# A decode step bound by its weight stream: new stream order, regrouped first layer of the MLP, smaller weight pieces, zero fill on VectorE, eight K/V buffers

## Chip, cores, metric

The kernel runs on one core of one Trainium2 chip. The metric is the device time of one execution in microseconds (us). Kernels that are compared ran on the same chip in alternating rounds. A ratio is the mean time of one kernel's fast runs over that of the other's of the same rounds, so it is not quite the ratio of the medians quoted beside it. The record calls a run faster or slower only beyond 2 %; a smaller difference is named below when its interval excludes 1.

In the profile lines PE is TensorE (the matmuls), DVE is VectorE, ACT ScalarE, POOL GpSimd, and SPq the queue in which the engine SP issues its loads (DMAs). PSUM is the memory, divided into banks, that matmuls add their results into.

## The reference, cut to what matters

```python
# one token, D = 576; 32 query heads, 16 K/V heads, Dh = 128; the last 4096 of 32768 cached positions
q = x @ wq                                   # 576 x 4096
p = softmax(q . K * Dh**-0.5)                # K: 16 heads x 4096 x 128
a = (p . V) @ wo                             # V the same; wo: 4096 x 576
b = gelu(x @ w1 + b1) @ w2 + b2              # w1: 576 x 4608, w2: 4608 x 576
out = g * a + (1 - g) * b                    # g = sigmoid(sum(x * gate_w))
```

There is one row of activations, so every weight and cache byte is used once: 53.6 MB are read, of which K and V are 33.6 MB and each of the four weight matrices about 5 MB.

## The kernel before

All large loads are issued by one engine (SP) in the order wq, K (16 tiles of 1 MiB), w1, V (16 tiles), wo, w2. K and V tiles share seven buffers. PE consumes wq (q), then each K tile (VectorE transposes it first), then, after the softmax, the MLP's first layer from w1, then V, then wo and w2 row by row.

```python
kv_pool = ctx.enter_context(tc.tile_pool(name="kv_pool", bufs=7, side="right"))
nc.gpsimd.memset(qz_flat, 0.0)                       # 128 x 8320 bf16
# ... q, then scores of 16 K tiles, softmax -> pt ...
first = True                                          # first layer of the MLP
for j in range(NJ):                                   # NJ = 18
    for half in range(2):
        col, f0 = half * NJ + j, half * FH + j
        for k in range(KM):                           # 4 matmuls, 128 rows of weights
            matmul(h_ps[:, col:col+1], lhsT=w1_m[:, k, f0:(half+1)*FH:NJ], rhs=xt[:, k:k+1], ...)
        matmul(h_ps[:, col:col+1], lhsT=b1_row[0:1, f0:(half+1)*FH:NJ], rhs=one_b, ...)   # bias: 1 row
    matmul(h_ps[:, j:NF:NJ], lhsT=w1_l[:, j:FH:NJ], rhs=xl[:, 0:2], ...)                  # last 64 rows of w1
for h in range(Hkv):                                  # V: load a tile, 32 matmuls of 2 columns
    ...
for r in range(0, RO, 16):                            # wo in two pieces
    nc.sync.dma_start(out=wo_t[:, r:r+16, :], in_=wo_src[:, r:r+16, :])
cuts = [(0, 0, 18), (1, 0, 9), (1, 9, 15), (1, 15, 18)]        # w2: rows per piece
# ... then one pair of matmuls (512 and 64 columns) for each of 32 rows of wo and 36 of w2, and
nc.scalar.copy(out=out_row[:, 320:D], in_=y_ps[0:1, 320:D])
nc.vector.tensor_copy(out=out_row[:, 0:320], in_=y_ps[0:1, 0:320])
nc.sync.dma_start(out=out, in_=out_row)
```

## Time and profile before

| | before |
|---|---|
| time, median | 144.57 us (144.55 to 144.71, 3 runs) |
| span of the profiled run | 142.9 us |
| bytes read, mean rate | 53.6 MB, 375 GB/s |
| PE, VectorE busy | 67 %, 39 % |
| last byte of w2 / end of the last matmul | 136.3 us (DMA records of the trace) / 139.4 us |

The page cuts the span into 40 slices, here of 3.57 us. The first line is the clock that TensorE was granted, in tenths; the second is what the DMA engines moved.

```profile
PEclk9999999999999999985555555555555555599998
...
GB/s 161 420 431 420 422 413 424 415 424 417 424 410 426 408 446 428 423 418 415 417 417 420 417 163 73 429 413 433 404 436 399 450 412 454 402 429 411 314 11 3
```

The stream runs at about 420 GB/s from the second slice on. Two things break it: slices 24 and 25 (163 and 73), the *hole*, and the *tail*, the last two slices, in which next to nothing is loaded. The shares of busy time say nothing of this: PE is busy 67 % of the span, but mostly in the shadow of the stream.

One caution about the clock line: the first clock record in the trace stands at 25.9 us, and where there is none the page shows 9. Before it TensorE was in fact at half clock: the 512-column matmuls of the K stage follow each other every 0.43 us up to 25.7 us, and every 0.22 us from 26.0 us on.

The view of what SP's queue waited for has the hole's cause (total us, times, longest):

```profile
SPq L342 <- PE o_ps L347: 22.9, 9, 16.3
```

Loads of V wait for PE to finish with a buffer, once for 16.3 us. What PE does in that time is the first layer. In PE's timeline (start, duration, engine, line, what) one group of columns looks so:

```profile
69.28 0.22 PE L304 MATMUL h_ps<-xl,w_t 128*128 128x2 bf16 x1
69.36 0.39 PE L287 MATMUL h_ps<-xt,w_t 128*128 128x1 bf16 x4
69.69 0.22 PE L296 MATMUL h_ps<-one_b,b_row 1*128 1x1 bf16 x1
69.83 0.41 PE L287 MATMUL h_ps<-xt,w_t 128*128 128x1 bf16 x4
70.17 0.22 PE L296 MATMUL h_ps<-one_b,b_row 1*128 1x1 bf16 x1
70.33 0.22 PE L304 MATMUL h_ps<-xl,w_t 128*128 128x2 bf16 x1
```

L287 is the loop over k, L296 the bias, L304 the last rows. A group of 11 matmuls repeats every 1.05 us (69.28 to 70.33), 18 times. The layer ends, V begins and the loads resume only here:

```profile
85.97 0.22 PE L304 MATMUL h_ps<-xl,w_t 128*128 128x2 bf16 x1
...
86.06 5.10 PE L347 MATMUL o_ps<-pt,kv_t 128*128 128x2 bf16 x186
...
87.08 3.74 SPq L342 DMA_DIRECT2D kv_t<-in_A_v_cache_dram  x5
```

The tail, in the chain that ended last (start, duration, what released what):

```profile
100.79 29.66 DMA w_t<-in_B_w_dram
130.49 0.38 PE y_ps L165
...
139.51 0.37 ACT out_row L390
139.90 0.48 DVE out_row L391
```

The first w2 piece (18 of 36 rows, 2.6 MB) lets PE go at 130.49 us; from there 36 row pairs of 0.245 us follow, then two copies and the store. The view of waits (total us, times, longest):

```profile
PE y_ps L165 <- DMA wo_t<-in_A_wo_dram: 3.4, 1, 3.4
...
PE y_ps L165 <- DMA w_t<-in_B_w_dram: 0.7, 1, 0.7
```

PE lost 3.4 us before its first row of wo, which came only with a piece of 16 rows, and 0.7 us before w2.

Last, two small VectorE copies beside the zero fill on GpSimd (busy us, mean ns | idle before):

```profile
L110 POOL MEMSET early<- 128x8320 bf16 x1 | 7.0, 7035 | 0.0
L120 DVE COPY xd<-x_row 1x64 bf16<-1x64 bf16 x2 | 6.0, 5908 | 1.0 <-DMA x_row<-in_A_x_dram 1.0
```

The Trainium skill, page "SBUF — State Buffer", section "SBUF: two separate sides", says that VectorE and GpSimd share one pair of ports as an exclusive lock: in some modes the later of two instructions waits for the whole of the other. The trace agrees: 64 elements took 5.9 us here, until 8.00 us, just after the fill's end at 7.92. That these copies were in such a mode is not shown by itself.

### The profile page before, as it was taken

What the parts mean: (1) busy time and instruction counts of PE and PEld (TensorE: products, weight loads), DVE (VectorE), ACT (ScalarE), POOL (GpSimd) and SP (SyncE); (2) the same over time, 40 slices, a digit from 0 to 9 for tenths busy, and PEclk for the clock granted to TensorE, in tenths of its full rate; (3) what the DMA queues carried; (4) which work ended last, traced back from release to release, by engine and by line L of the source; (5) the groups of instructions that cost most, each with busy time, mean ns of one, the idle gap of its engine ahead of it and who ended that gap; (6) DMA issues with size and microseconds to landing.
All of it is one profiled execution on the core that took longest, in us unless ns stands there. A gap on an engine that the chain in (4) does not pass through costs nothing.

```text
span 142.9 us, 2520 instructions
## 1 busy us (share of the span) xinstructions
PE 95.9 (67%) x1140; PEld 60.2 (42%) x1140; DVE 55.8 (39%) x82; ACT 3.8 (3%) x8; POOL 7.7 (5%) x7
## 2 busy tenths in 40 slices
PE   0049639988867868624999999933342507998990
PEld 0034513333323323213899999933342502343440
DVE  4968297899998989446000004000000030000001
ACT  3000000000000000020000000000000000000001
POOL 8920000000000000000000000000000000000000
PEclk9999999999999999985555555555555555599998
DMA  4999999999999999999999933999999999999700
GB/s 161 420 431 420 422 413 424 415 424 417 424 410 426 408 446 428 423 418 415 417 417 420 417 163 73 429 413 433 404 436 399 450 412 454 402 429 411 314 11 3
DMA packets 6645, 53.79 MB, mean 376 GB/s; under 512 B 741, under 2 KB 745, under 8 KB 1257
## 3 DMA queue, kind: packets, MB, share of 16 engines
q1 hardware_dynamic: 6626, 53.61, 90.5%
q8 instruction: 9, 0.15, 0.4%
q14 instruction: 2, 0.02, 0.0%
q10 hardware_dynamic: 8, 0.01, 0.0%
HBM read 53.62 MB, written 0.00 MB: 375 GB/s over the span
## 4 chain that ended last, share of the span: by engine, by line
DMA 57%; PE 30%; DVE 10%; issue 1%; ACT 1%; ACTq 0%
DMA w_t<-in_B_w_dram 38%; DMA kv_t<-in_A_k_cache_dram 10%; DMA kv_t<-in_A_v_cache_dram 8%; PE h_ps L287 7%; PE y_ps L165 7%; PE s_ps L228 4%; DVE xd L120 4%; PE h_ps L296 4%; DVE early L224 3%; PE o_ps L347 2%; PE h_ps L304 2%; PE q_ps L178 2%; PE y_ps L168 1%; DMA x_row<-in_A_x_dram 1%; DVE junk_row L135 0%
## 5 line engine op out<-in xcount | busy, mean ns | idle before, releaser
L228 PE MATMUL s_ps<-early 128*128 128x512 bf16 x128 | 32.8, 403 | 10.5 <-DVE early L224 10.5
L224 DVE STREAM_TRANSPOSE early<-kv_t 128x2048 f32<-128x2048 f32 x16 | 36.6, 2304 | 3.7 <-DMA kv_t<-in_A_k_cache_dram 2.1
L228 PEld LDWEIGHTS <-early 128*128 128x128 bf16 x128 | 12.9, 101 | 30.0 <-issue 17.9
L347 PE MATMUL o_ps<-pt,kv_t 128*128 128x2 bf16 x512 | 15.2, 165 | 13.0 <-DMA kv_t<-in_A_v_cache_dram 10.4
L347 PEld LDWEIGHTS <-kv_t 128*128 128x128 bf16 x512 | 14.5, 104 | 13.7 <-DMA kv_t<-in_A_v_cache_dram 10.9
L287 PE MATMUL h_ps<-xt,w_t 128*128 128x1 bf16 x144 | 14.5, 204 | 1.7 <-DMA w_t<-in_B_w_dram 1.7
L165 PE MATMUL y_ps<-wo_t,ov 128*1 128x512 bf16 x32 | 10.9, 470 | 3.4 <-DMA wo_t<-in_A_wo_dram 3.4
L287 PEld LDWEIGHTS <-w_t 128*128 128x128 bf16 x144 | 12.3, 160 | 2.0 <-DMA w_t<-in_B_w_dram 1.8
L371 DVE COPY o_sb<-o_ps 128x32 f32<-128x32 f32 x1 | 0.2, 192 | 25.8 <-PE o_ps L347 25.8
L391 DVE CAST out_row<-y_ps 1x320 bf16<-1x320 f32 x1 | 0.5, 478 | 24.1 <-ACT out_row L390 24.1
L165 PE MATMUL y_ps<-w_t,gt 128*1 128x512 bf16 x36 | 9.0, 380 | 0.7 <-DMA w_t<-in_B_w_dram 0.7
L296 PE MATMUL h_ps<-one_b,b_row 1*128 1x1 bf16 x36 | 7.8, 217 | 0.0
L313 DVE COPY hacc<-h_ps 128x36 f32<-128x36 f32 x1 | 0.2, 195 | 18.5 <-PE h_ps L304 18.5
L110 POOL MEMSET early<- 128x8320 bf16 x1 | 7.0, 7035 | 0.0
L168 PE MATMUL y_ps<-wo_t,ov 128*1 128x64 bf16 x32 | 6.9, 217 | 0.0
L168 PE MATMUL y_ps<-w_t,gt 128*1 128x64 bf16 x36 | 6.9, 193 | 0.0
L120 DVE COPY xd<-x_row 1x64 bf16<-1x64 bf16 x2 | 6.0, 5908 | 1.0 <-DMA x_row<-in_A_x_dram 1.0
L165 PEld LDWEIGHTS <-ov 128*1 128x1 bf16 x32 | 3.2, 100 | 6.6 <-issue 3.8
L296 PEld LDWEIGHTS <-b_row 1*128 1x128 bf16 x36 | 4.9, 135 | 0.5
L165 PEld LDWEIGHTS <-gt 128*1 128x1 bf16 x36 | 3.0, 84 | 4.7
L304 PE MATMUL h_ps<-xl,w_t 128*128 128x2 bf16 x18 | 4.0, 223 | 0.5 <-DMA w_t<-in_B_w_dram 0.5
L168 PEld LDWEIGHTS <-ov 128*1 128x1 bf16 x32 | 3.0, 94 | 3.0 <-issue 3.0
(75 smaller groups left out, 39.4 us busy)
## 6 DMA issues: line engine op xcount, KB each, us to landing
kv_t<-in_A_k_cache_dram SPq DMA_DIRECT2D x16, 1024.0 KB, 15.3
kv_t<-in_A_v_cache_dram SPq DMA_DIRECT2D x16, 1024.0 KB, 18.9
w_t<-in_B_w_dram SPq DMA_DIRECT2D x2, 2304.0 KB, 20.5
wo_t<-in_A_wo_dram SPq DMA_DIRECT2D x2, 2304.0 KB, 25.9
wq_t<-in_A_wq_dram SPq DMA_DIRECT2D x4, 1024.0 KB, 7.9
w_t<-in_B_w_dram SPq DMA_DIRECT2D x1, 2592.0 KB, 29.7
w_t<-in_B_w_dram SPq DMA_DIRECT2D x1, 1296.0 KB, 30.3
w_t<-in_B_w_dram SPq DMA_DIRECT2D x1, 864.0 KB
```

The source lines that it names most:

```text
L110: nc.gpsimd.memset(qz_flat, 0.0)
L120: nc.vector.tensor_copy(out=xd[:, :, t], in_=x_row[0:1, DM:D])
L165: nc.tensor.matmul(y_ps[0:1, 0:N0], lhsT=vec, rhs=row[:, 0:N0], start=start, stop=stop, skip_group_check=True)
L168: nc.tensor.matmul(y_ps[0:1, N0:D], lhsT=vec, rhs=row[:, N0:D], start=start, stop=stop, skip_group_check=True)
L178: nc.tensor.matmul(q_ps[:, j : j + 1], lhsT=wq_m[:, k, j * Dh : (j + 1) * Dh], rhs=xt[:, k : k + 1], start=(k == 0 and j == 0), stop=False ...
L224: nc.vector.transpose(out=kt.bitcast(FP32), in_=k_t[:].bitcast(FP32))
L228: nc.tensor.matmul(s_ps[:, f * 512 : (f + 1) * 512].rearrange("p (c k) -> p c k", k=32), lhsT=qz[:, h, j, :], rhs=kv[:, f * 16 : (f + 1) * ...
L287: nc.tensor.matmul(h_ps[:, col : col + 1], lhsT=w1_m[:, k, f0 : (half + 1) * FH : NJ], rhs=xt[:, k : k + 1], start=first, stop=False, skip ...
L296: nc.tensor.matmul(h_ps[:, col : col + 1], lhsT=b1_row[0:1, f0 : (half + 1) * FH : NJ], rhs=one_b[0:1, 0:1], start=False, stop=False, skip ...
L304: nc.tensor.matmul(h_ps[:, j:NF:NJ], lhsT=w1_l[:, j:FH:NJ], rhs=xl[:, 0:2], start=False, stop=(j == NJ - 1), skip_group_check=True,)
L347: nc.tensor.matmul(o_ps[:, 2 * h : 2 * h + 2], lhsT=v_t[:, c, :], rhs=pt[:, c, 2 * h : 2 * h + 2], start=(c == 0), stop=(c == NCH - 1),)
L391: nc.vector.tensor_copy(out=out_row[:, 0:320], in_=y_ps[0:1, 0:320])
```

## The change

Its intent is to keep the stream full: the first layer moves to where PE has nothing else to do, V follows the softmax at once, and the last pieces are small so that little work is left after the last byte. There are several edits at once.

1. Stream order w1, wq, K, V, wo, w2, and the first layer is computed first.
2. w1 in four pieces and a rest, wo in four pieces in place of two, w2 in six in place of four.
3. The loop nest of the first layer is regrouped: all 36 bias matmuls, then for each k all 36 columns, then the 18 of the last rows.
4. The zero fill goes from GpSimd to VectorE.
5. Eight K/V buffers. wo and w2 take over other tiles (tags A and B in place of C and A), which makes room.

```diff
-    kv_pool = ... bufs=7
+    kv_pool = ... bufs=8
+    for k in range(KM):                                   # before wq now
+        nc.sync.dma_start(out=w1_m[:, k, :], in_=w1_src[:, k, :])
-    nc.gpsimd.memset(qz_flat, 0.0)
+    nc.vector.memset(qz_flat.bitcast(FP32), 0.0)
+    for c in range(NF):                                   # before q now; 36 columns
+        f0 = (c // NJ) * FH + c % NJ
+        matmul(h_ps[:, c:c+1], lhsT=b1_row[0:1, f0:(c//NJ+1)*FH:NJ], rhs=one_b, start=(c == 0), ...)
+    for k in range(KM):
+        for c in range(NF):
+            matmul(h_ps[:, c:c+1], lhsT=w1_m[:, k, f0:(c//NJ+1)*FH:NJ], rhs=xt[:, k:k+1], ...)
+    for j in range(NJ):
+        matmul(h_ps[:, j:NF:NJ], lhsT=w1_l[:, j:FH:NJ], rhs=xl[:, 0:2], ...)
     ... (gelu as before; the old nest and the old loads of w1 go) ...
-    for r in range(0, RO, 16):
+    for r in range(0, RO, 8):
-    cuts = [(0, 0, 18), (1, 0, 9), (1, 9, 15), (1, 15, 18)]
+    cuts = [(0, 0, 9), (0, 9, 18), (1, 0, 8), (1, 8, 13), (1, 13, 16), (1, 16, 18)]
```

More of the change, by code (lines that the diff above doesn't have):

```diff
@@ L52 @@
     big = ctx.enter_context(tc.tile_pool(name="big", bufs=1, side="right"))
-    kv_pool = ctx.enter_context(tc.tile_pool(name="kv_pool", bufs=7, side="right"))
+    kv_pool = ctx.enter_context(tc.tile_pool(name="kv_pool", bufs=8, side="right"))
     ps_s = ctx.enter_context(tc.tile_pool(name="ps_s", bufs=1, space=bass.MemoryType.PSUM))
@@ L68 @@
     nc.scalar.dma_start(out=b1_row[:], in_=B_b1.rearrange("(o n) -> o n", o=1))
+    w1_t = big.tile([P, KM * F + FH], BF16, name="w1_t", tag="B")
+    w1_m = w1_t[:, 0 : KM * F].rearrange("p (k n) -> p k n", k=KM)
+    w1_l = w1_t[:, KM * F :]
+    w1_src = B_w1[0:DM, :].rearrange("(p k) n -> p k n", k=KM)
+    for k in range(KM):
+        nc.sync.dma_start(out=w1_m[:, k, :], in_=w1_src[:, k, :])
+    nc.sync.dma_start(out=w1_l, in_=B_w1[DM:D, :].rearrange("r (two n) -> (r two) n", two=2))
     wq_t = big.tile([P, KM * Hq * Dh + QH], BF16, name="wq_t", tag="A")
@@ L172 @@
     y_add(one_f[0:1, 0:1], b2g[0:1, :], start=True)
+    h_ps = ps_h.tile([P, NF], FP32, name="h_ps")
+    for c in range(NF):
+        f0 = (c // NJ) * FH + c % NJ
+        nc.tensor.matmul(
+            h_ps[:, c : c + 1],
+            lhsT=b1_row[0:1, f0 : (c // NJ + 1) * FH : NJ],
+            rhs=one_b[0:1, 0:1],
+            start=(c == 0),
+            stop=False,
+            skip_group_check=True,
+        )
+    for k in range(KM):
+        for c in range(NF):
+            f0 = (c // NJ) * FH + c % NJ
+            nc.tensor.matmul(
+                h_ps[:, c : c + 1],
+                lhsT=w1_m[:, k, f0 : (c // NJ + 1) * FH : NJ],
+                rhs=xt[:, k : k + 1],
+                start=False,
+                stop=False,
+                skip_group_check=True,
+            )
+    for j in range(NJ):
+        nc.tensor.matmul(
+            h_ps[:, j:NF:NJ],
+            lhsT=w1_l[:, j:FH:NJ],
+            rhs=xl[:, 0:2],
+            start=False,
+            stop=(j == NJ - 1),
+            skip_group_check=True,
+        )
+    hacc = const.tile([P, NF], FP32, name="hacc")
+    nc.vector.tensor_copy(out=hacc[:], in_=h_ps[:])
+    z2 = const.tile([P, NF], FP32, name="z2")
+    nc.vector.tensor_tensor(out=z2[:], in0=hacc[:], in1=hacc[:], op=ALU.mult)
+    C0 = 0.7978845608028654
+    poly = const.tile([P, NF], FP32, name="poly")
+    nc.vector.tensor_scalar(
+        out=poly[:],
+        in0=z2[:],
+        scalar1=2.0 * C0 * 0.044715,
+        scalar2=2.0 * C0,
+        op0=ALU.mult,
+        op1=ALU.add,
+    )
+    u_t = const.tile([P, NF], FP32, name="u_t")
+    nc.vector.tensor_tensor(out=u_t[:], in0=poly[:], in1=hacc[:], op=ALU.mult)
+    e_h = const.tile([P, NF], FP32, name="e_h")
+    nc.scalar.activation(out=e_h[:], in_=u_t[:], func=ACT.Exp, scale=-1.0)
+    nc.vector.tensor_scalar(out=e_h[:], in0=e_h[:], scalar1=1.0, scalar2=None, op0=ALU.add)
+    r_t = const.tile([P, NF], FP32, name="r_t")
+    nc.vector.reciprocal(out=r_t[:], in_=e_h[:])
+    p1 = const.tile([P, NF], FP32, name="p1")
+    nc.vector.tensor_tensor(out=p1[:], in0=hacc[:], in1=r_t[:], op=ALU.mult)
+    gt = const.tile([P, NF], BF16, name="gt")
+    nc.vector.tensor_scalar(out=gt[:], in0=p1[:], scalar1=omg[:, 0:1], scalar2=None, op0=ALU.mult)
     q_ps = ps_m.tile([P, Hq], FP32, name="q_ps", tag="m")
@@ L235 @@
                 )
-    w1_t = big.tile([P, KM * F + FH], BF16, name="w1_t", tag="B")
-    w1_m = w1_t[:, 0 : KM * F].rearrange("p (k n) -> p k n", k=KM)
-    w1_l = w1_t[:, KM * F :]
-    w1_src = B_w1[0:DM, :].rearrange("(p k) n -> p k n", k=KM)
-    for k in range(0, KM, 2):
-        nc.sync.dma_start(out=w1_m[:, k : k + 2, :], in_=w1_src[:, k : k + 2, :])
-    nc.sync.dma_start(out=w1_l, in_=B_w1[DM:D, :].rearrange("r (two n) -> (r two) n", two=2))
     m1 = const.tile([P, 1], FP32, name="m1")
@@ L277 @@
     nc.vector.transpose(out=pt[:].rearrange("p c h -> p (c h)"), in_=p_t[:])
-    h_ps = ps_h.tile([P, NF], FP32, name="h_ps")
-    first = True
-    for j in range(NJ):
-        for half in range(2):
-            col = half * NJ + j
-            f0 = half * FH + j
-            for k in range(KM):
-                nc.tensor.matmul(
-                    h_ps[:, col : col + 1],
-                    lhsT=w1_m[:, k, f0 : (half + 1) * FH : NJ],
-                    rhs=xt[:, k : k + 1],
-                    start=first,
-                    stop=False,
-                    skip_group_check=True,
-                )
-                first = False
-            nc.tensor.matmul(
-                h_ps[:, col : col + 1],
-                lhsT=b1_row[0:1, f0 : (half + 1) * FH : NJ],
-                rhs=one_b[0:1, 0:1],
-                start=False,
-                stop=False,
-                skip_group_check=True,
-            )
-        nc.tensor.matmul(
-            h_ps[:, j:NF:NJ],
-            lhsT=w1_l[:, j:FH:NJ],
-            rhs=xl[:, 0:2],
-            start=False,
-            stop=(j == NJ - 1),
-            skip_group_check=True,
-        )
@@ L312 @@
-    hacc = const.tile([P, NF], FP32, name="hacc")
-    nc.vector.tensor_copy(out=hacc[:], in_=h_ps[:])
-    z2 = const.tile([P, NF], FP32, name="z2")
-    nc.vector.tensor_tensor(out=z2[:], in0=hacc[:], in1=hacc[:], op=ALU.mult)
-    C0 = 0.7978845608028654
-    poly = const.tile([P, NF], FP32, name="poly")
-    nc.vector.tensor_scalar(
-        out=poly[:],
-        in0=z2[:],
-        scalar1=2.0 * C0 * 0.044715,
-        scalar2=2.0 * C0,
-        op0=ALU.mult,
-        op1=ALU.add,
-    )
-    u_t = const.tile([P, NF], FP32, name="u_t")
@@ L327 @@
-    nc.vector.tensor_tensor(out=u_t[:], in0=poly[:], in1=hacc[:], op=ALU.mult)
-    e_h = const.tile([P, NF], FP32, name="e_h")
-    nc.scalar.activation(out=e_h[:], in_=u_t[:], func=ACT.Exp, scale=-1.0)
-    nc.vector.tensor_scalar(out=e_h[:], in0=e_h[:], scalar1=1.0, scalar2=None, op0=ALU.add)
-    r_t = const.tile([P, NF], FP32, name="r_t")
-    nc.vector.reciprocal(out=r_t[:], in_=e_h[:])
-    p1 = const.tile([P, NF], FP32, name="p1")
-    nc.vector.tensor_tensor(out=p1[:], in0=hacc[:], in1=r_t[:], op=ALU.mult)
@@ L335 @@
-    gt = const.tile([P, NF], BF16, name="gt")
-    nc.vector.tensor_scalar(out=gt[:], in0=p1[:], scalar1=omg[:, 0:1], scalar2=None, op0=ALU.mult)
     o_ps = ps_o.tile([P, Hq], FP32, name="o_ps")
@@ L356 @@
     RO = Hq * Dh // P
-    wo_t = big.tile([P, RO, D], BF16, name="wo_t", tag="C")
+    wo_t = big.tile([P, RO, D], BF16, name="wo_t", tag="A")
     wo_src = A_wo.rearrange("(p r) n -> p r n", r=RO)
-    for r in range(0, RO, 16):
-        nc.sync.dma_start(out=wo_t[:, r : r + 16, :], in_=wo_src[:, r : r + 16, :])
-    w2_t = big.tile([P, NF, D], BF16, name="w2_t", tag="A")
+    for r in range(0, RO, 8):
+        nc.sync.dma_start(out=wo_t[:, r : r + 8, :], in_=wo_src[:, r : r + 8, :])
+    w2_t = big.tile([P, NF, D], BF16, name="w2_t", tag="B")
     w2_src = B_w2.rearrange("(b p j) n -> p b j n", b=2, j=NJ)
-    cuts = [(0, 0, 18), (1, 0, 9), (1, 9, 15), (1, 15, 18)]
+    cuts = [(0, 0, 9), (0, 9, 18), (1, 0, 8), (1, 8, 13), (1, 13, 16), (1, 16, 18)]
     for b, j0, j1 in cuts:
```

## The prediction

> **What bounds it now.** The weight and cache stream. The page's slices show about 420 GB/s from 4 to 132 us (53.6 MB, the 16 DMA engines full). The rest of the 142.9 us span is a start of 2 us, one hole, and a tail.
> - Hole: slices 24 and 25 (82 to 89 us) show 163 and 73 GB/s; (677 / 420) x 3.57 = 5.1 us of stream lost (estimate). In the SP waits V loads wait for PE on o_ps (22.9 us, longest 16.3). PE is in the MLP's first layer from 66.8 to 86.0 us (timeline: 11 matmuls per 1.04 us), consumes no V tile, all 7 buffers fill, loads stop.
> - Tail: the DMA records end at 136.3 us, but the first 2.6 MB piece of w2 releases PE only at 130.49 (chain of waits). 36 row pairs at 0.245 us then run PE-bound to 139.4; copies and store take 3.45 us more.
>
> **What the change does.**
> 1. The first layer moves to the front, in the stream's shadow. PE passes straight from softmax to V. With V0 finished near 81 us and V7 landing near 86, V8 is issued in time: the hole closes, -5.1 us.
> 2. w2 lands in six pieces, the last of 3 and 2 rows. PE's 0.245 us a row beats the stream's (147 KB / 420 GB/s = 0.35 us), so only the last rows remain after the last byte: 0.5 us to the first matmul (first w2 piece: bytes end 129.98, matmul 130.49), then about 0.6. This tail shrinks from 3.1 us to 1.1: -2.0 us.
> 3. VectorE's zero fill replaces GpSimd's 7.04 us memset, beside which two VectorE copies of 64 elements took 5.98 us (line groups). x is ready 3 to 5 us sooner; not critical.
> 4. Added delay: q comes after w1. PE first does 36 bias matmuls (0.14 us each), 144 strided ones (0.083) and the fp32 bias row (2.1): q is ready at 32 to 34 us, though wq lands at 26. K starts 4 us behind, but a backlogged K tile needs 2.19 us, the stream 2.5, and eight buffers hold 20 us. It is absorbed; K ends at 71 to 73 us.
> 5. Bytes and matmuls are the same.
>
> The Trainium skill, "TensorE: Matmul & The Clock Gate", Part 1, says that an idle PE falls to half clock and takes a busy window to return. The trace agrees: granted clock 0.5 from 63.4 to 124.8 us; one- and two-column matmuls did not lift it, it rose 5.9 us after the 512-column wo matmuls began (0.48 us a row before, 0.245 after). This stays: wo starts near 109 us, falls 12 rows behind, and catches up by 125, before the bytes end.
>
> **Sum.** Stream end 136.3 - 5.1 = 131.2 us; +0.5 landing, +0.6 matmuls, +3.45 end = 135.8 us span. Times are 1.7 us above the span: 137.5 us, 0.951 of before. Range 136.0 to 139.6. Chances: faster by over 2% 0.94, within 2% 0.05, slower 0.01.
>
> **Right if:** slices from 4 to 129 us are all near 420 GB/s; V loads wait little on PE; the chain ends in w2's DMA, two to five rows, copies; K transposes start at 32 to 36 us.
>
> **Wrong if:** V0 ends after 86 us (a smaller hole returns); PE stays at half clock into w2 (up to 5 us more); small last pieces slow the stream or land unevenly over the 16 engines.

## The result and the profile after

| | before | after |
|---|---|---|
| time, median | 144.64 us (144.55 to 144.91, 4 runs) | 137.97 us (137.96 to 138.04, 4 runs) |
| ratio | | 0.9537 (95 % interval 0.9521 to 0.9554) |
| span | 142.9 us | 136.1 us |
| mean rate | 375 GB/s | 394 GB/s |
| last byte of w2 / end of the last matmul | 136.3 / 139.4 us | 131.7 / 133.2 us |

The span is 6.8 us shorter. The last byte comes 4.6 us earlier (the hole), and from the last byte to the end of the last matmul it is 1.5 us in place of 3.1 (the tail). The same two lines of slices, now of 3.40 us:

```profile
PEclk9999999999999999999999655555555555799999
...
GB/s 122 423 425 421 420 419 419 408 420 412 421 421 424 419 417 421 419 417 424 419 421 414 419 421 424 412 421 412 417 421 414 427 427 406 433 417 426 403 182 0
```

No slice between the second and the 38th is under 403 GB/s. SP's longest wait for PE on V is now 10.2 us, in a time in which enough loads are queued already:

```profile
SPq L341 <- PE o_ps L346: 14.3, 8, 10.2
```

The start of the program, all engines:

```profile
7.71 2.39 PE L187 MATMUL h_ps<-one_b,b_row 1*128 1x1 bf16 x36 [0.25 <-DMA b_row<-in_B_b_dram]
...
10.03 4.64 PE L198 MATMUL h_ps<-xt,w_t 128*128 128x1 bf16 x72
...
16.61 4.64 PE L198 MATMUL h_ps<-xt,w_t 128*128 128x1 bf16 x72
...
21.11 1.26 PE L207 MATMUL h_ps<-xl,w_t 128*128 128x2 bf16 x18
...
22.23 1.84 PE L245 MATMUL q_ps<-xt,wq_t 128*128 128x1 bf16 x64
...
27.35 1.01 PE L245 MATMUL q_ps<-xt,wq_t 128*128 128x1 bf16 x32 [1.69 <-DMA wq_t<-in_A_wq_dram]
...
30.95 2.31 DVE L291 STREAM_TRANSPOSE early<-kv_t 128x2048 f32<-128x2048 f32 x1 [0.41 <-DMA kv_t<-in_A_k_cache_dram]
```

The layer's matmuls are the same 198, but 36, 72, 72 and 18 of them take 2.39, 4.64, 4.64 and 1.26 us, 12.9 us in all; before, 18 groups of 1.05 us took 18.9. The last part of q waits for wq until 27.35 us, so the layer does not delay q: the first K tile is transposed at 30.95. V:

```profile
80.34 5.26 PE L346 MATMUL o_ps<-pt,kv_t 128*128 128x2 bf16 x192 [2.59 <-DVE pt L335]
...
85.84 1.01 PE L346 MATMUL o_ps<-pt,kv_t 128*128 128x2 bf16 x32 [0.23 <-DMA kv_t<-in_A_v_cache_dram]
```

At 80.34 us PE starts on six V tiles that have landed meanwhile (192 matmuls in one go); from 85.84 it waits for each tile. The tail:

```profile
105.85 22.70 DMA w_t<-in_B_w_dram
...
128.59 0.38 PE y_ps L174
...
133.20 0.37 ACT out_row L389
...
133.60 0.48 DVE out_row L390
```

The piece of eight w2 rows lands and lets PE go at 128.59 us; the chain is PE from there on. Its 18 row pairs (8 + 5 + 3 + 2) never wait again.

The fill and the copies of x (busy us, mean ns | idle before):

```profile
L140 DVE MEMSET early<- 128x4160 f32 x1 | 3.5, 3525 | 0.8 <-issue 0.8
...
L127 DVE COPY xd<-x_row 1x64 bf16<-1x64 bf16 x2 | 0.2, 154 | 0.0
```

The fill now takes 3.5 us of VectorE itself, so x comes only 1.5 us earlier (the cast of x^T ends at 6.9 us in place of 8.4).

PE's clock behaves as in the kernel before. Two stretches (length, busy us and instructions of PE, weight loads, VectorE, ScalarE, GpSimd; then granted clock, DMA share, GB/s):

```profile
111.00:117.00 6.00, 5.83 (x25) 2.25 (x25) 0.00 (x0) 0.00 (x0) 0.00 (x0) 0.50 1.01 416
117.00:123.00 6.00, 5.37 (x45) 2.40 (x43) 0.00 (x0) 0.00 (x0) 0.00 (x0) 0.99 1.03 429
```

The first wo matmul starts at 111.17 us at half clock; six us later the full clock is back, and by 121.9 us PE has caught up with the stream and waits for w2.

### The profile page after: what moved, and what is told of

Read it like the earlier page. It is cut to its first block, busy times and chain, and to the rows that moved or that the text cites. A ratio compares the mean times of both kernels' runs of the same rounds, so it can differ in the third digit from the quotient of the medians.

```text
span 136.1 us, 2522 instructions
## 1 busy us (share of the span) xinstructions
PE 90.0 (66%) x1140; PEld 54.9 (40%) x1140; DVE 53.4 (39%) x83; ACT 3.8 (3%) x8; POOL 0.7 (1%) x6
## 4 chain that ended last, share of the span: by engine, by line
DMA 77%; DVE 9%; PE 9%; issue 2%; SPq 1%; ACT 0%; DVEq 0%
DMA kv_t<-in_A_v_cache_dram 27%; DMA kv_t<-in_A_k_cache_dram 27%; DMA w_t<-in_B_w_dram 24%; DVE early L291 9%; PE s_ps L295 5%; PE y_ps L174 3%; PE o_ps L346 1%; SPq L76 1%; PE y_ps L177 0%; DVE out_row L390 0%; ACT out_row L389 0%; DVEq L291 0%
## 5 line engine op out<-in xcount | busy, mean ns | idle before, releaser
L295 PEld LDWEIGHTS <-early 128*128 128x128 bf16 x128 | 12.8, 100 | 29.9 <-issue 16.3
L174 PE MATMUL y_ps<-wo_t,ov 128*1 128x512 bf16 x32 | 10.9, 471 | 0.6 <-DMA wo_t<-in_A_wo_dram 0.6
L198 PE MATMUL h_ps<-xt,w_t 128*128 128x1 bf16 x144 | 9.3, 201 | 0.0
L198 PEld LDWEIGHTS <-w_t 128*128 128x128 bf16 x144 | 9.1, 167 | 0.2 <-issue 0.2
L245 PE MATMUL q_ps<-xt,wq_t 128*128 128x1 bf16 x128 | 3.9, 165 | 2.3 <-DMA wq_t<-in_A_wq_dram 2.3
L174 PEld LDWEIGHTS <-gt 128*1 128x1 bf16 x36 | 3.0, 84 | 4.8
L245 PEld LDWEIGHTS <-wq_t 128*128 128x128 bf16 x128 | 3.7, 105 | 2.4 <-DMA wq_t<-in_A_wq_dram 2.4
L177 PEld LDWEIGHTS <-gt 128*1 128x1 bf16 x36 | 3.0, 84 | 2.1 <-issue 2.1
L140 DVE MEMSET early<- 128x4160 f32 x1 | 3.5, 3525 | 0.8 <-issue 0.8
L187 PE MATMUL h_ps<-one_b,b_row 1*128 1x1 bf16 x36 | 2.4, 196 | 0.3 <-DMA b_row<-in_B_b_dram 0.3
```

Of the source, the lines that this page charges most:

```text
L140: nc.vector.memset(qz_flat.bitcast(FP32), 0.0)
L174: nc.tensor.matmul(y_ps[0:1, 0:N0], lhsT=vec, rhs=row[:, 0:N0], start=start, stop=stop, skip_group_check=True)
L177: nc.tensor.matmul(y_ps[0:1, N0:D], lhsT=vec, rhs=row[:, N0:D], start=start, stop=stop, skip_group_check=True)
L187: nc.tensor.matmul(h_ps[:, c : c + 1], lhsT=b1_row[0:1, f0 : (c // NJ + 1) * FH : NJ], rhs=one_b[0:1, 0:1], start=(c == 0), stop=False, sk ...
L198: nc.tensor.matmul(h_ps[:, c : c + 1], lhsT=w1_m[:, k, f0 : (c // NJ + 1) * FH : NJ], rhs=xt[:, k : k + 1], start=False, stop=False, skip_ ...
L245: nc.tensor.matmul(q_ps[:, j : j + 1], lhsT=wq_m[:, k, j * Dh : (j + 1) * Dh], rhs=xt[:, k : k + 1], start=(k == 0 and j == 0), stop=False ...
```

## The experiments

Labels with b_ change the kernel before, those with a_ the changed one. All outputs were correct. In each table the last column is against the kernel before in the same rounds.

### First set: the hole and the tail, one part at a time

The theory was that the hole comes from PE being kept in the first layer while buffers fill. Rivals: the eighth buffer closes it; the layer is quicker in the changed kernel because of its place; small pieces gain nothing.

```diff
 b_8buf:       -bufs=7  +bufs=8        (and wo, w2 on tiles A and B)
 b_grouped:    old loop nest -> new loop nest, still after the softmax
 a_oldpieces:  wo in 2 pieces, w2 cut as before
 a_7buf:       -bufs=8  +bufs=7
```

> The kernel before with eight K/V buffers in place of seven (wo and w2 moved to the tiles that the changed kernel uses, else it does not fit), nothing else. Theory A (the hole comes from PE being in the first layer while buffers fill): one more 1.05 MB tile is loaded into the hole, 2.5 us of it is filled, 2.6 us stay; about 142.1 us, -2.5. Rival B (the eighth buffer is what closes the hole): no hole, about 139.5 us.

> The kernel before with only the loop nest of the first layer replaced by the changed kernel's one (36 bias matmuls first, then 36 per k, then the 18 of the last rows), still after the softmax. Theory A (in the changed trace the 198 matmuls took about 13 us in place of 19 because matmuls of equal row count follow each other): they take about 13 us here too, V0 is consumed near 81 us, the hole shrinks from 5.1 us to at most 0.3; about 139.7 us. Rival B (they were quicker because of where they stand: clock, or what PE and the SBUF do at that time): still 19 us, hole and time unchanged at 144.6 us.

> The changed kernel with wo in 2 and w2 in 4 pieces as before. Theory A: no hole, the stream ends at about 131.7 us as in the changed kernel, but the first w2 piece of 2.6 MB lands about 6 us before the end and 36 row pairs at 0.245 us follow it: PE ends 3.0 us after the last byte in place of 1.5; about 139.4 us, +1.5 against the changed kernel. Rival B (small pieces gain nothing since PE catches up anyway): 138.0 us.

> The changed kernel with seven K/V buffers. Theory A (order closes the hole): V0 is consumed at 81.4 us, the seventh V tile lands at 83.5, so the stream has 2 us of slack or nearly: 138.0 to 138.4 us. Rival B (the eighth buffer is needed): a hole of up to 2.5 us, up to 140.5 us.

| run | median us | before us | ratio (95 %) |
|---|---|---|---|
| b_8buf | 142.28 | 144.63 | 0.984 (0.983 to 0.986) |
| b_grouped | 139.68 | 144.63 | 0.968 (0.963 to 0.974) |
| a_oldpieces | 139.90 | 144.63 | 0.968 (0.966 to 0.969) |
| a_7buf | 137.94 | 144.63 | 0.954 (0.952 to 0.955) |

The eighth buffer fills one tile's worth of the hole when there is a hole (2.4 us; the low slices are now 25 and 26, with 238 and 327):

```profile
GB/s 136 426 429 420 422 415 415 420 420 425 415 415 422 418 415 439 446 425 394 419 427 408 420 418 238 327 420 429 418 415 442 425 420 421 461 384 414 290 4 0
```

and is worth nothing in the changed kernel. The old pieces cost 1.9 us there, a little more than the 1.5 expected. The pieces of wo and of w2 were not changed apart. In a_oldpieces PE waited 3.5 us for its first wo row, and 0.8 us for the first w2 piece, which came at 125.60 us. From these waits (estimates): smaller w2 pieces alone could save at most 0.8 us, and smaller wo pieces alone nothing, since PE would then wait for the same w2 piece. It takes both.

The surprise is b_grouped (one of its four runs took 141.3 us, which makes its interval wide; b_biasfirst below has one such run too, 141.1 us). One loop nest, left in its old place, with the old stream order, seven buffers and the old pieces, takes 5.0 of the 6.7 us. There is no hole:

```profile
GB/s 133 424 425 421 426 415 418 420 423 413 420 418 420 413 420 449 433 427 398 416 420 416 420 418 413 420 413 418 420 413 430 443 421 431 445 406 407 296 2 3
```

Its timeline shows why it is even earlier than expected:

```profile
62.93 4.62 PE L294 MATMUL h_ps<-xt,w_t 128*128 128x1 bf16 x72
...
67.84 4.62 PE L294 MATMUL h_ps<-xt,w_t 128*128 128x1 bf16 x72
...
72.32 1.28 PE L303 MATMUL h_ps<-xl,w_t 128*128 128x2 bf16 x18
...
73.46 1.84 PE L346 MATMUL o_ps<-pt,kv_t 128*128 128x2 bf16 x64
```

Three things come together. The matmuls take 64 ns each. The scheduler has moved the bias matmuls, which need no w1, to 10.9 us, long before. And with k outermost the first 72 need only the first w1 piece, so they run in the gap of the softmax, from 62.9 us on. PE reaches V at 73.5 us in place of 86.1.

So the rival "it is the place" fell for the speed of the layer. But it also shook the reading of the change: is the new order of the stream worth anything?

### Second set: order without the nest, the fill, and what is slow in the old nest

```diff
 a_interleaved:  new loop nest -> old loop nest (first in the program)
 a_orderonly:    the same, and bufs=7, fill on GpSimd, old pieces of wo and w2
                 (w1 still in four pieces and a rest, wo and w2 on tiles A and B)
 a_gpsimdfill:   fill back on GpSimd
 b_biasfirst:    kernel before; 36 bias matmuls first, then the old nest without them
```

> The changed kernel with the old loop nest of the first layer (per column group 4 + bias + 4 + bias + 1 of the last rows), still first in the program. Theory A (it is the nest that makes the layer cost 13 or 19 us, and the nest that ties its start to the last piece of w1): it starts in earnest when the last w1 piece lands near 16 us, takes 19 us, q is ready near 40 instead of 29, K ends near 79 instead of 73, V0 is consumed near 87.5, after V7 lands at 86: a hole of about 2.5 us, 140.5 us. Rival B (being first in the stream is what counts, the slack absorbs the rest): 138.0 us.

> Only the new order of stream and first layer: old loop nest, seven buffers, GpSimd fill, old pieces of wo and w2. Theory A: V0 is consumed near 87.5 us while the seventh V tile lands at 83.5 to 84, so a hole of about 5 us, as in the kernel before, and the long tail: about 144.9 us, no gain. Rival B (order is the gain): about 140 us.

> The changed kernel with the zero fill back on GpSimd. Theory A: the two small VectorE copies beside it take 6 us again, x is ready near 8.3 in place of 6.8 us, q at 29 to 30.5 since PE had 2.3 us of waits on wq to spare; K is at most 1.5 us later and the slack before V8 (V0 consumed 81.4, V7 landed 86) takes it: 138.0 us. Rival B (the fill is part of the gain): over 138.7 us.

> The kernel before with only the 36 bias matmuls (one row of weights) taken out of the nest and put first; the other 162 keep the old order, four in a row on the same PSUM column. Theory A (each change between one-row and 128-row weights costs PE about 80 ns): the 162 take 65 ns each, 10.5 us in all, from about 68 to 79 us, V0 consumed near 80 us, hole at most 0.3 us; about 139.8 us. Rival B (four accumulations in a row on one PSUM column are what is slow): 95 ns each, 15.5 us, V0 consumed near 85 us, a hole of 3 us left; about 142.5 us.

| run | median us | before us | ratio (95 %) |
|---|---|---|---|
| a_interleaved | 141.84 | 144.79 | 0.981 (0.979 to 0.983) |
| a_orderonly | 146.15 | 144.79 | 1.010 (1.005 to 1.016) |
| a_gpsimdfill | 138.10 | 144.79 | 0.954 (0.953 to 0.955) |
| b_biasfirst | 139.62 | 144.79 | 0.967 (0.962 to 0.972) |

The new order alone is 1 % *slower* than the kernel before (the interval excludes 1, and its fastest run, 145.60 us, is above all runs of the kernel before). The hole is back at the same place in the slices, and there is a second, shallow one in the K stage:

```profile
GB/s 143 426 423 419 429 423 405 421 423 419 414 421 326 337 369 414 362 403 428 428 419 421 419 355 52 398 419 416 428 416 414 455 417 433 412 435 403 301 11 3
```

With the changed kernel's other parts kept, the old nest still costs 3.9 us (against the kernel before the record calls a_interleaved unclear, as its interval lies on both sides of 2 %):

```profile
GB/s 122 420 425 417 428 420 420 417 420 417 415 415 420 420 408 356 392 429 417 424 422 422 415 410 401 143 422 424 415 415 420 428 422 413 421 417 425 408 148 0
```

In a_interleaved PE begins with V at 87.24 us and frees the first buffer at 88.3. By the landings in the trace the seventh V tile had landed at 86.2 us and the eighth, the last that had a buffer, landed at 88.7; the ninth, issued at 88.3, came at 93.0. The first layer had to wait for the last piece of w1 (16.3 us), and then took 18 us before q. The V hole was expected (2.5 us); the weak slices 16 and 17 were not: the first K tile was transposed only at 41 us, so K buffers came free late as well. From the slices' shortfall against 420 GB/s (estimate) they cost 0.9 us, the larger part of the 1.3 us by which the expectation was too low. In a_orderonly, with seven buffers, the weak slices of the K stage cost 2.7 us and the hole 3.9 in place of the 5 expected; the time was 1.2 us over the expectation.

The fill gives nothing: 0.954 with it on GpSimd and 0.954 without, though the two copies take 6 us again.

b_biasfirst settles what is slow in the old nest. It keeps the order of the old nest, four matmuls in a row on one PSUM column and one of two columns after every eight, and takes out the bias alone:

```profile
68.68 0.20 PE L304 MATMUL h_ps<-xl,w_t 128*128 128x2 bf16 x1
68.74 0.64 PE L296 MATMUL h_ps<-xt,w_t 128*128 128x1 bf16 x8
69.24 0.20 PE L304 MATMUL h_ps<-xl,w_t 128*128 128x2 bf16 x1
69.30 0.64 PE L296 MATMUL h_ps<-xt,w_t 128*128 128x1 bf16 x8
...
77.75 0.40 PE L347 MATMUL o_ps<-pt,kv_t 128*128 128x2 bf16 x10
```

A group is now nine matmuls in 0.56 us (68.68 to 69.24), 62 ns each, as in the regrouped nest. The rival of four accumulations in a row on one column would have had 95 ns. So two bias matmuls in a group cost 1.05 - 0.56 = 0.49 us, 0.24 us each, where 36 in a row take 0.066 each. What is slow is not the bias matmul, but going back and forth between one-row weights and 128-row weights: (0.49 - 2 x 0.066) / 4 changes = 0.09 us for each change. What PE does in that time no view shows; that it is the number of rows, rather than some other property of that operand, is the likely reading and was not tested by itself.

The Trainium skill, page "TensorE: Matmul & The Clock Gate", section "LDWEIGHTS (loading the stationary operand)", says that a weight load takes as long for 32 rows as for 128. The trace agrees for loads in a row (66 ns a matmul with one row, 64 with 128); the cost of changing between them is what it does not have.

### Third set: the same time with fewer edits, and a better version

```diff
 b_grouped_pieces:  kernel before with the new loop nest and the small pieces, nothing else
 a_fine:            -(1, 0, 8), (1, 8, 13), (1, 13, 16), (1, 16, 18)
                    +(1, 0, 7), (1, 7, 12), (1, 12, 15), (1, 15, 17), (1, 17, 18)
 a_halves:          -N0 = 512, columns 512 to 575 in the next PSUM bank; copies of 256 and 320 columns
                    +N0 = 288, 288 columns in each bank; ScalarE copies one bank, VectorE the other
 a_halves_fine:     both
```

> The kernel before with two edits: the new loop nest of the first layer (still after the softmax) and the small pieces of wo and w2. The order of the stream, the seven buffers and the GpSimd fill stay as before. Theory A (the nest closes the hole and the pieces shorten the tail; the order of the stream gives nothing by itself): 139.7 less the 1.9 us that the pieces gave the changed kernel, about 137.9 us, level with the changed kernel. Rival B (the new order is needed for the last part of the gain): 138.6 us or more.

> The changed kernel with the second half of w2 in 7, 5, 3, 2, 1 rows in place of 8, 5, 3, 2. In the changed trace PE never waits after the piece of 8 lands: its 18 row pairs end 1.5 us after the last byte. Theory A (PE-bound from that piece on): the piece of 7 lands 0.35 us later with 11 rows of 0.35 us behind it, and PE ends about 0.25 us earlier: 137.7 us. Rival B (the last byte decides): no change, 138.0 us.

> The changed kernel with the output row in two halves of 288 columns in two PSUM banks in place of 512 and 64. In the changed trace VectorE's copy of 320 columns starts only when ScalarE's of 256 has ended (0.36 and 0.48 us in a row). Theory A: the copies run side by side, the end is 0.4 us shorter, a row pair stays at 0.245 us: 137.6 us. Rival B (two 288-column matmuls cost more than 512 and 64, or the copies still go one after the other): 138.0 us or more.

> Both of the last two edits together. If they are independent: 0.65 us less than the changed kernel, about 137.35 us.

| run | median us | before us | ratio (95 %) |
|---|---|---|---|
| b_grouped_pieces | 137.68 | 144.54 | 0.952 (0.951 to 0.954) |
| a_fine | 137.81 | 144.54 | 0.953 (0.952 to 0.954) |
| a_halves | 137.95 | 144.54 | 0.955 (0.953 to 0.956) |
| a_halves_fine | 137.23 | 144.54 | 0.950 (0.948 to 0.951) |

Two edits of the kernel before give all of the change's gain: 0.952, level with the changed kernel's 0.954. The order of the stream, the eighth buffer and the fill are not needed for it.

a_fine alone is 0.16 us quicker by the medians, in the direction of the 0.25 expected, but within the interval. a_halves alone gave nothing. The copies do run side by side, but the store came late (timeline):

```profile
133.08 0.45 DVE L390 CAST out_row<-y_ps 1x288 bf16<-1x288 f32 x1 [22.25 <-PE y_ps L174]
133.20 0.39 ACT L389 CAST out_row<-y_ps 1x288 bf16<-1x288 f32 x1 [56.12 <-PE y_ps L177]
133.98 0.31 SPq L391 DMA_DIRECT2D out_dram<-out_row  x1
```

ScalarE's copy ends at 133.59, and SP issues the store only at 133.98. With the finer pieces too, it follows at once:

```profile
132.78 0.45 DVE L390 CAST out_row<-y_ps 1x288 bf16<-1x288 f32 x1 [21.97 <-PE y_ps L174]
132.90 0.39 ACT L389 CAST out_row<-y_ps 1x288 bf16<-1x288 f32 x1 [55.73 <-PE y_ps L177]
133.31 0.32 SPq L391 DMA_DIRECT2D out_dram<-out_row  x1
```

Copies end at 133.29, the store goes at 133.31. The ratio is 0.950 against the changed kernel's 0.954, 0.6 us of 144.6, and the two intervals do not overlap; by the medians, on different chips, it is 0.74 us. That is about the 0.65 expected for both edits, but they are not independent: in the same rounds a_halves gave nothing by itself and 0.6 us on top of a_fine. Its four runs lie between 137.85 and 138.04 us, so the profiled gap in front of the store is no odd execution. The views show nothing that SP waited for in that gap, but SP's own instruction records tell more. In all 14 traces SP's 80th recorded instruction starts at least 0.39 us after the end of the 79th: by 0.39 to 0.43 us in seven of them, and in the other seven somewhere within a longer wait for other work. 0.6 to 0.9 us after such a visible pause, or 3.5 to 4.0 us into the wait, the trace has an 8 KB read by a DMA queue of kind "instruction". In a_halves the 80th instruction is the store itself (133.56 to 133.98). In a_halves_fine SP issues one load more, so that the 80th is the wait for the copies, and the pause is hidden. So a_halves lost to the pause what the parallel copies gained. That SP sets off a fetch of its next instructions there is the likely reading; it was not tested by itself. a_halves_fine is the fastest version, faster than both kernels.

That the copies may overlap at all agrees with the Trainium skill, page "PSUM — Partial Sum Buffer", section "Specifications (TRN2)": ScalarE and VectorE can read PSUM in parallel as long as they are in different banks. In the changed kernel both copies touch the first bank, and the second copy was made to wait for the first (133.20 + 0.36, then 133.60).

## Why the prediction was right

The time was 137.97 us against 137.5, within the range, and the two terms that carry the gain were right. Point by point:

- **Hole, -5.1 us: right in size and in how it closes.** All slices are full. V0 was consumed at 81.4 us (predicted 81). V6, the seventh tile, landed at 85.8 us and V7 at 88.5, 2.5 us later than predicted, so the slack was 7 us in place of 5; with seven buffers, as in a_7buf, some 4 us are left, which is why the eighth is worth nothing there. The credit was incomplete: step 1 puts it down to the layer's place, and step 5 counts the matmuls as the same. The runs show that the place alone does not close the hole (a_orderonly, 146.15 us), that the regrouped nest alone does (b_grouped, 139.68 us), and that with the old nest in the new place V0 is consumed after 88 us (a_interleaved), which is the prediction's own condition for being wrong.
- **Tail, -2.0 us: 3.1 became 1.5, not 1.1, so -1.6.** The step assumed that PE keeps up and only the last rows are left. PE was still busy without a break from the piece of eight rows on, so that the end was that piece's landing and 18 row pairs. a_oldpieces measures the pieces at 1.9 us: in the traces the last matmul ends 1.4 us later, and the rest of the end is 0.6 us longer, mostly SP's pause (third set).
- **x ready 3 to 5 us sooner: 1.5 us.** The fill itself holds VectorE from 1.84 to 5.36 us. It is off the critical path, as said (a_gpsimdfill).
- **q at 32 to 34 us: 29 us.** The costs per matmul (0.14 and 0.083 us) were read from the interleaved nest, where they contain the changes between bias and weights; in the new nest they are 0.066 and 0.064. The delay was not only absorbed but absent: PE waited 2.3 us for wq. This is the same oversight as in step 5.
- **Clock: right.** wo started at 111.2 us (109 predicted), half clock for six us, caught up by 122.
- **Sum.** Stream end 131.7 (131.2), matmuls 1.5 us after it (1.1), end 2.9 us after those (3.45). In the kernel before SP's pause of 0.39 us falls behind the store, where it counts; in the changed kernel SP's 80th instruction is the store, which it reaches during the wait for PE, and the pause is hidden. The prediction knew nothing of this, so part of the match is luck: the first two terms were 0.9 us too low, and the end was 0.55 us too high.
- **Two of its "right if" points missed.** K transposes started at 30.95 us, not at 32 to 36, and the chain ends in 18 row pairs, not in two to five.

| part of the change | alone, on the kernel before | taken out of the changed kernel |
|---|---|---|
| regrouped nest | -5.0 us (b_grouped) | +3.9 us (a_interleaved) |
| small pieces of wo and w2 | not run alone; -2.0 us after the nest (b_grouped to b_grouped_pieces) | +1.9 us (a_oldpieces) |
| eighth buffer | -2.4 us (b_8buf) | 0 (a_7buf) |
| zero fill on VectorE | not run | 0 (a_gpsimdfill) |
| new order, with w1 in smaller pieces | +1.4 us (a_orderonly) | 0 (b_grouped_pieces, which lacks the eighth buffer and the new fill too) |

The columns don't add up, and shouldn't: a hole can only be closed once. The 2.0 in the second row compares the differences from the kernel before of two sets on different chips.

## What to carry to other kernels

When a stream has a hole, find the engine that holds its buffers and look at how long its work takes and why, before moving that work: here a regrouped loop nest was worth 5.0 us and moving it without regrouping made the kernel 1 % slower. Keep matmuls with one-row weights (biases) out of runs of full ones, and put the loop that matches the pieces of a load outermost, so that a scheduler can start on the first piece. Size the last pieces so that the engine behind the stream is never more than one small piece behind, and price an instruction from a trace only for the neighbours that it had there.

## What the Trainium skill lacked or had wrong

- "TensorE: Matmul & The Clock Gate": nothing on the cost of alternating between one-row and 128-row weights, 0.09 us for each change here: 0.24 us for a bias matmul between full ones, 0.066 in a row.
- The same page, "Weight-path perf modes": it allows a step between columns for the fast load, and neither it nor the skill's general warning on strided reads has a figure for weights. With a step of 18 elements 72 matmuls took 4.64 us (64 ns each), with contiguous columns 64 took 1.84 us (29 ns each), in the same trace between 10 and 24 us. The step was not tested by itself.
- The same page, Part 1: it has a busy PE warm up. Here 18 us of back-to-back matmuls of one and two columns did not lift the half clock (0.50 from 63.4 to 124.8 us before); 512-column matmuls did in 5.3 to 6.0 us, in the K stage and with wo, in both kernels.
- "DMA: Bandwidth & Descriptors", "Rules for kernel authors", asks for at least 1 MiB per DMA for full bandwidth. With several in the queue, pieces of 0.3 to 0.7 MB at the end of the stream did not slow it by more than 0.3 us: the last byte came at 131.7 us in the changed kernel, at 131.4 with the old pieces (a_oldpieces; the first of 2.6 MB, the last two of 0.9 and 0.4) and at 131.4 with still smaller ones (a_fine), by the DMA records of the traces.
- No page has the length of SP's pause before its 80th recorded instruction: 0.39 to 0.43 us in seven traces, hidden in a wait in the other seven.
